# The first seven iterations of an attention and routing kernel, written out by hand

## The chip, the cores and the metric

The kernel runs on one core of a Trainium2 chip. The metric is the device time of one execution in microseconds (us), on the slowest core, here the only one. Five engines work side by side, each in the order of its own instruction stream: TensorE (PE in the rows, its weight loads PEld), VectorE (DVE), ScalarE (ACT), GpSimd (POOL), and SyncE (SP), which only issues DMAs. An instruction waits until what it reads is written and until the buffer it writes is free, and all behind it on its engine wait with it.

## The reference

Three layers run one after another. The change touches only the first, attention over pooled keys and values, for 8 batches of 8 heads, 576 tokens and 64 elements a head:

```python
k_p = k.reshape(B, H, Sp, pool, D).mean(axis=3)      # pool 8: 576 rows become 72
v_p = v.reshape(B, H, Sp, pool, D).mean(axis=3)
scores = scale * np.matmul(q, k_p.transpose(0, 1, 3, 2))
scores = scores - np.max(scores, axis=-1, keepdims=True)
attn = np.exp(scores)
attn = attn / (np.sum(attn, axis=-1, keepdims=True) + 1e-09)
attn_out = np.matmul(attn, v_p).astype(np.float32)
...
xn = x / (np.linalg.norm(x, axis=-1, keepdims=True) + 1e-06)
en = expert_emb / (np.linalg.norm(expert_emb, axis=-1, keepdims=True) + 1e-06)
logits = xn @ en.T / tau
expert_idx = np.argmax(logits, axis=1)
...
h = np.maximum(np.maximum(x @ w1, x @ w2), x @ w3)
out = h @ w_out
```

Its output, 4608 tokens of 512 elements, is routed: each token goes to the one expert of eight with the largest logit (a product with the normalised expert embedding `en`) and is weighted by a softmax over the logits. A dense layer follows.

## The kernel before

**Tiles and loop.** The tokens are cut into 36 tiles of 128, nine for two batches (four of the even batch, one mixed tile with half of each, four of the odd batch). The loop `for it in range(NT + 4)` (line 1607) runs a software pipeline over them. Its iteration `it` issues, in this order: the loads that are due; scores, maximum and subtraction of tile it-1 (`stage_s`, 449 to 491); the turned weights of tile it-3 (`stage_a`, 496: five transposes on TensorE, two copies on ScalarE); the turned queries of tile `it` (`stage_q`, 434, copied by ScalarE); the exponent of tile it-1 (`stage_e`, 492); the squares for the token's norm that are waiting in `squares` (line 557, ScalarE); the value products of tile it-4 and the output behind them on VectorE (`stage_x`, 516 to 557: reciprocal of the sum, the scaled output `x`, the logits `dt` and `lg`); and last the jobs that the table `todo` has for this iteration. All products are in fp32 and take two passes on TensorE.

**Keys and values.** `prep_steps(b)` (297) gives the jobs that prepare one batch. The raw rows lie as 72 x 8 = 576 rows in five chunks (four of 128 partitions, one of 72). The eight rows behind a pooled one are added, on VectorE by one reduction of a chunk (`pool_k`, 305; `pool_v1`, 313) or on GpSimd by three halving additions (`pool_k2`, 319; `pool_v`, 329). `dup_k` (323, ScalarE) copies the key sums beside themselves, `trans_k` (342) turns them on TensorE, and ScalarE copies them into a block `kbd` with zeros beside them (351, 352), one of three in turn. `spread_v` (335, GpSimd) writes the value sums into a block `vbd`, `trans_v` (372) turns them, and `vdot` (379, 386) multiplies them with the expert embedding, so that the value products yield the logits too. From batch 2 on the values lie beside the keys in the tile `kp`, and one transposition turns both (`trans_kv`, 359, with the copies 365 to 367).

**Loads.** `load_rows` (214) loads a batch's raw rows on SP's queue, `load_half` (204) half of them, and `add_half` (212) adds the other half to them by accumulating DMAs on GpSimd's queue, from batch 3 on. The raw tiles have one tag each, `kraw` and `vraw`, that hands its buffers round.

**What sets the order at the start.** Before the loop stand the key sums of batch 0 and their turning (`p0[0]()`, 1505). The norm of the expert embedding (`en_steps`, 1506) and constants for the routing (`const_steps`, 1545) are generators: `between` and `fill` draw one step of them at a time from a queue, in the gaps of VectorE's stream. The jobs of batches 0 to 2 are spread over the iterations by hand:

```python
todo = {0: [lambda: fill(16), p0[2]], 1: [lambda: fill(2), p0[3]], 2: [p0[4]], 3: [p0[5]], 5: [...const_steps...]}
at_ = {1: [2, 4, 6, 7], 2: [5, 6, 6, 7, 7, 7, 8, 9, 10]}.get(b, at_[:4] + at_[5:6])
```

So batch 2's first key sum goes out in iteration 5, the next two in 6, the last two and the spreading and turning from 7 on; batch 3's accumulating loads go out in iteration 4.

Of the kernel before, what the change touches and what calls it, by code (L numbers as in the profile page):

```python
# [21 lines left out]
def attention_moe_moe_kernel(  # L22
# [97 lines left out]
    if True:  # L120
# [61 lines left out]
        if True:  # L182
# [31 lines left out]
            def load_rows(pool_tag, src, b, sizes, apart=False, step=4):  # L214
                t = kvp.tile([P, 5, J, D], F32, tag=pool_tag, name=f"{pool_tag}{b}")
# [74 lines left out]
            for c, (h0, h1) in enumerate(HS[:4]):  # L290
                nc.gpsimd.tensor_copy(mslot[:, SL[c] : SL[c + 1], 0], rmask[:, c, h0:h1])
            for i in range(3):
                if i > 0:
                    nc.gpsimd.memset(kbds[i], 0.0)
                nc.gpsimd.tensor_scalar(vbds[i][:, :, D : D + 1], mslot, float(J), None, A.mult)

            def prep_steps(b):
# [8 lines left out]

                def pool_all():
                    for c in range(5):
                        pool_k(c)
# [20 lines left out]

                def spread_v():
                    for c, (h0, h1) in enumerate(HS):
                        n = RC[c]
                        sh = [n, h1 - h0, D]
                        nc.gpsimd.tensor_tensor(
                            vb[0:n, SL[c] : SL[c + 1], 0:D],
                            vp[0:n, c : c + 1, :].to_broadcast(sh),
                            mslot[0:n, SL[c] : SL[c + 1], :].to_broadcast(sh),
                            op=A.mult,
                        )  # L340

                def trans_k(cs, h0, h1):
# [50 lines left out]
                if b == 0:  # L393
                    return [
                        lambda: (pool_all(), dup_k(), trans_k(range(4), 0, 7), trans_k([4], 7, 8)),
                        lambda: (pool_v(2, 4, P), pool_v(4, 5, R4)),
                        lambda: pool_v1(0),
                        lambda: (pool_v1(1), spread_v()),
                        lambda: (trans_v(0, 4), trans_v(4, 5)),
                        lambda: vdot(),  # L400
                    ]
                if b == 1:
                    return [
                        lambda: (pool_k(0), pool_k(1), pool_k2(RC, 2), pool_v(0, 4, P), pool_v(4, 5, R4)),
                        lambda: (dup_k(), spread_v(), trans_k(range(4), 0, 7), trans_k([4], 7, 8)),
                        lambda: (trans_v(4, 5), trans_v(0, 4)),
                        vdot,
                    ]
# [25 lines left out]
            def stage_q(i):  # L434
# [4 lines left out]
                for c in range(4):  # L439
# [5 lines left out]
                    nc.tensor.transpose(ps[:, c * P : (c + 1) * P], blk_, ident)  # L445
                nc.scalar.copy(qT, ps.rearrange("p (c n) -> p c n", n=P))
                st_q[i] = qT

            def stage_s(i):
                m, part, t, segs = tiles[i]  # L450
                qT = st_q.pop(i)
                ps = pb.tile([P, 2, 512], F32, tag="psc", name=f"psc{i}")
                if part == 1:
# [62 lines left out]
            def stage_x(i):  # L516
                m, part, t, segs = tiles[i]
                aT = st_a.pop(i)
                ps = pb.tile([P, 2, 512], F32, tag="pav", name=f"pav{i}")
                for bank in range(2):  # L520
# [53 lines left out]
            uses = {}  # L574

            def uname(name):
                uses[name] = uses.get(name, 0) + 1
                return f"{name}_{uses[name]}"

# [924 lines left out]
            nc.scalar.activation(esq, en, AF.Square, accum_out=ess)  # L1504
            p0[0]()
            def en_steps():
                en2 = yield from inverse_norm(ap1, ess, E, 1, "en")
                vs(en, en, en2[:, 0:1], A.mult)
                yield
                ps = pq.tile([P, 512], F32, tag="pq", name="pe0")  # L1510
# [75 lines left out]

            queue.append([chain(en_steps())])
# [13 lines left out]
            qneed = {0: 0, 1: 4, 2: 5}  # L1601
            qnext = 3
            kvnext = 2
            cur = {}
            MA = NT1 + 3
            first = run(range(NREQ), between)
            for it in range(NT + 4):
                boundary()
# [9 lines left out]
                if it == NT:  # L1618
                    sq_.close()
                    open_b()  # L1620
                while qnext < len(qorder) and qorder[qnext][0] * 9 + qneed[qorder[qnext][1]] - 4 <= it:
                    load_q(*qorder[qnext])
                    qnext += 1
                while kvnext < B and kvnext * 4.5 - 11 <= it:
                    if kvnext < NFULL:
                        kv[kvnext] = (load_rows("kraw", k, kvnext, RC), load_rows("vraw", v, kvnext, RC))
                    else:
                        kv[kvnext] = (load_half("kraw", k, kvnext), load_half("vraw", v, kvnext))
                    kvnext += 1
                if 0 <= it - 1 < NT:  # L1630
# [15 lines left out]
                if it == NT + 1:  # L1646
                    next(first)
                for job in todo.get(it, []):
                    if callable(job):
                        job()  # L1650
                        continue
                    b, j = job
                    if b not in cur:
                        cur[b] = prep_steps(b)
                    cur[b][j]()
                if it == NT - 1 and started:
# [350 lines left out]
```

## Time and profile before

| | before |
|---|---|
| runs, median of 3 | 1204.89 us (1204.51 to 1204.91) |
| the profiled execution, its own time | 1203.55 us |
| its span, first to last instruction | 1201.4 us |
| mean granted clock of TensorE (1 is full) | 0.997 |
| TensorE busy | 1175.2 us (98%) |
| VectorE busy | 873.2 us (73%) |
| ScalarE busy | 606.8 us (51%) |
| GpSimd busy | 297.4 us (25%) |

The time of an execution is 2.15 us longer than its span. The attention covers only the start of the span, and the edited iterations some 50 us of it; an average over the span says nothing of them, so what matters there is read from timelines and short stretches. Busy time of TensorE is modelled at the ends of its matmuls, and grouped rows of matmuls overlap their neighbours a little; from one start to the next is the better measure of what a group takes.

### The profile page before, as it was taken

To read this page: it belongs to the slowest core of one execution; us is meant where nothing else is said; L and a number is where in the kernel's file an instruction comes from. 1 tells how busy PE (TensorE), PEld (TensorE's weight loads), DVE (VectorE), ACT (ScalarE), POOL (GpSimd) and SP (SyncE) were. 2 spreads that over 40 slices of the span, in tenths; PEclk is the share of its full clock that TensorE was granted. 3 is DMA by queue.
4 is the path that set the end of the run, shared out by engine and by line. 5 is a ranking of instruction groups with operands and counts; after the bars stand their busy time and mean duration, and the time that the engine had idled before them with its cause. 6 is when DMAs were issued, how large, how long until landed. Compare 5 with 4: busy or idle time off the path is not lost.

```text
span 1201.4 us, 23859 instructions
## 1 busy us (share of the span) xinstructions
PE 1175.2 (98%) x8761; PEld 1161.6 (97%) x8761; DVE 873.2 (73%) x1811; ACT 606.8 (51%) x1118; POOL 297.4 (25%) x462
## 2 busy tenths in 40 slices
PE   5999999999999999999999999999999999999997
PEld 4899999999999999999999999999999999999997
DVE  6878977978799999988765468468467557567563
ACT  4667674545666666666655244334334334334332
POOL 7978634001222122221201301103104004004001
PEclk9999999999999999999999999999999999999999
DMA  9899656328874457554939668877878877878873
GB/s 294 238 270 253 175 172 220 111 21 239 268 251 177 153 176 238 200 206 135 345 110 323 231 252 302 302 263 290 318 258 287 307 271 281 298 287 284 287 258 141
DMA packets 108121, 285.11 MB, mean 237 GB/s; under 512 B 17879, under 2 KB 70565, under 8 KB 97629
## 3 DMA queue, kind: packets, MB, share of 16 engines
q1 hardware_dynamic: 87436, 216.40, 51.8%
q0 software_dynamic: 20560, 67.11, 17.9%
q8 instruction: 71, 1.16, 0.4%
q14 instruction: 54, 0.43, 0.1%
HBM read 285.52 MB, written 52.48 MB: 281 GB/s over the span
## 4 chain that ended last, share of the span: by engine, by line
PE 92%; DVE 3%; ACT 2%; issue 1%; POOL 0%; DMA 0%; SPq 0%; POOLq 0%; DVEq 0%; ACTq 0%
PE p L1752 33%; PE ph L1097 17%; PE py L1158 17%; PE o L1864 10%; PE pav L524 3%; PE psc L470 2%; PE ph L1105 2%; PE py L1142 2%; PE px L1051 1%; PE paT L501 1%; PE pqT L445 1%; DVE sh L488 1%; DVE kp L305 1%; PE pd L379 1%; POOL out_dram L1872 0%
## 5 line engine op out<-in xcount | busy, mean ns | idle before, releaser
L1752 PE MATMUL p<-yhi,wt 128*128 128x384 f32 x1512 | 387.4, 336 | 0.1
L1752 PEld LDWEIGHTS p<-yhi,wt 128*128 128x128 f32 x1512 | 273.4, 188 | 0.3 <-issue 0.3
L1752 PE MATMUL p<-ylo,wt 128*128 128x384 f32 x756 | 254.1, 336 | 0.0
L1760 ACT COPY s<-p 128x384 f32<-128x384 f32 x162 | 77.6, 479 | 200.7 <-PE p L1752 200.7
L1158 PE MATMUL py<-hhi,whi 128*128 128x256 f32 x576 | 164.6, 286 | 0.0
L1097 PE MATMUL ph<-xhi,wlo 128*128 128x256 f32 x576 | 163.1, 283 | 0.5 <-DVE wlo L1077 0.5
L1097 PE MATMUL ph<-xhi,whi 128*128 128x256 f32 x576 | 163.5, 284 | 0.0
L1097 PE MATMUL ph<-xlo,whi 128*128 128x256 f32 x576 | 163.0, 283 | 0.0
L1158 PE MATMUL py<-hhi,wlo 128*128 128x256 f32 x576 | 162.9, 283 | 0.0
L1158 PE MATMUL py<-hlo,whi 128*128 128x256 f32 x576 | 162.9, 283 | 0.0
L1752 PEld LDWEIGHTS p<-ylo,wt 128*128 128x128 f32 x756 | 142.2, 188 | 0.0
L1864 PE MATMUL o<-wt,ghi 128*128 128x256 f32 x756 | 136.2, 282 | 0.0
L1779 DVE TENSOR_TENSOR blk<-p,s 128x384 f32<-128x384 f32 x108 | 59.6, 552 | 88.8 <-PE p L1752 88.8
L1737 POOL DMA_INDIRECT gt<-gbuf,ix x26 | 33.9, 1304 | 337.9 <-DMA ix<-idbuf 267.9
L1864 PEld LDWEIGHTS o<-wt,ghi 128*128 128x128 f32 x756 | 116.7, 188 | 0.9 <-DVE m L1780 0.8
L1097 PEld LDWEIGHTS ph<-xhi,wlo 128*128 128x128 f32 x576 | 110.5, 192 | 0.7 <-DVE wlo L1077 0.7
L1097 PEld LDWEIGHTS ph<-xhi,whi 128*128 128x128 f32 x576 | 110.5, 192 | 0.0
L1097 PEld LDWEIGHTS ph<-xlo,whi 128*128 128x128 f32 x576 | 110.5, 192 | 0.0
L1158 PEld LDWEIGHTS py<-hlo,whi 128*128 128x128 f32 x576 | 110.5, 192 | 0.0
L1158 PEld LDWEIGHTS py<-hhi,whi 128*128 128x128 f32 x576 | 110.4, 192 | 0.0
L1158 PEld LDWEIGHTS py<-hhi,wlo 128*128 128x128 f32 x576 | 110.4, 192 | 0.0
L1077 DVE TENSOR_TENSOR wlo<-w2raw,whi 128x1024 fp32r<-128x1024 f32 x86 | 105.1, 1225 | 6.9 <-ACT whi L1068 6.8
(345 smaller groups left out, 2348.6 us busy)
## 6 DMA issues: line engine op xcount, KB each, us to landing
wt<-wdram SPq DMA_DIRECT2D x69, 1792.0 KB
w1raw<-in_moe_w_dram SPq DMA_DIRECT2D x88, 512.0 KB
w2raw<-in_moe_w_dram SPq DMA_DIRECT2D x88, 512.0 KB
wdram<-wst POOLq DMA_DIRECT2D x9, 1792.0 KB, 6.6
ybuf<-yo SPq DMA_DIRECT2D x40, 256.0 KB
cvraw<-in_moe_w_dram POOLq DMA_DIRECT2D x36, 256.0 KB, 4.4
xbuf<-x SPq DMA_DIRECT2D x16, 512.0 KB
yr<-ybuf SPq DMA_DIRECT2D x20, 384.0 KB
```

The lines of the kernel that those rows point to most:

```text
L470: nc.tensor.matmul(ps[:, c // 2, (c % 2) * 2 * SP : (c % 2 + 1) * 2 * SP], qT[:, c, :], kbds[segs[0][2] % 3][:, h0 + c].rearrange("p t s - ...
L524: nc.tensor.matmul(ps[lo:hi, bank, (g0 % 4) * DA : (g0 % 4 + g1 - g0) * DA], aT[:, c, lo:hi], vbds[b % 3][:, sl : sl + g1 - g0, :].rearran ...
L1077: nc.vector.tensor_tensor(lo, src, hi.bitcast(F32), op=A.subtract)
L1097: nc.tensor.matmul(ps[:, f, :], a_[:, c, fs], b_[:, c, :], start=(n == 0), stop=(n == 3 * DC - 1))
L1105: nc.tensor.matmul(ps[:, f, 0:P], tl["w1"][piece][:, c, fs], xlo[:, c, 0:P], start=(c == 0), stop=(c == DC - 1))
L1142: nc.tensor.matmul(ps[h], a_[:, f, 0:P], b_[:, f, cols], start=(piece == 0 and f == 0 and n == 0), stop=(last_ and f == 1 and n == 2),)
L1158: nc.tensor.matmul(py[:, c // 2, (c % 2) * 256 : (c % 2 + 1) * 256], a_[:, f, c * P : (c + 1) * P], b_[:, f, :], start=(piece == 0 and f = ...
L1737: nc.gpsimd.indirect_dma_start(out=gt[g][:, j : j + 1], out_offset=None, in_=gbuf[:, :], in_offset=bass.IndirectOffsetOnAxis(ap=cols[j], a ...
L1752: nc.tensor.matmul(ps, a_, b_, start=(start and c + n == 0), stop=(c == 1 and n == 2), skip_group_check=True)
L1760: nc.scalar.copy(t, ps)
L1779: tt(src, add[0], add[1], op=A.add)
L1864: nc.tensor.matmul(ps, a_, b_, start=(m in (1, 2, 5) and c + n == 0), stop=(c == KH - 1 and n == 2), skip_group_check=True,)
```

## The change

The loop now begins at iteration 8. Iterations 0 to 7 are written out as straight calls, in another order: tiles 0 and 2 are scored first, then 1 and 3; the query copy of tile 0 goes to VectorE; the steps of the embedding norm are issued between the key sums of batch 0; GpSimd adds chunks 1 and 4 of batch 0's keys, VectorE the fifth value chunk of batch 0; batch 1's sums and products come at other places. A new helper `turn(n)` issues n products of the identity with itself, whose result nothing reads. Batch 2's key sums go out two with tile 6's iteration and three in iteration 8, its turned keys in 9; batch 3's accumulating loads in iteration 8; the routing constants from iteration 11. On SP's queue the keys of batch 1 stand before the mixed queries, its values before the third group of queries. The raw tiles have tags by even and odd batch, with one buffer each.

```diff
-                t = kvp.tile([P, 5, J, D], F32, tag=pool_tag, name=f"{pool_tag}{b}")
+                t = kvp.tile([P, 5, J, D], F32, tag=f"{pool_tag}{b % 2}", name=f"{pool_tag}{b}_", bufs=1)
...
+            kv[1] = [load_rows("kraw", k, 1, RC)]
             load_q(0, 1)
-            kv[1] = [load_rows("kraw", k, 1, RC)]
+            kv[1].append(load_rows("vraw", v, 1, RC))
             load_q(0, 2)
-            kv[1].append(load_rows("vraw", v, 1, RC))
...
+            def turn(n):
+                ps = pb.tile([P, 2, 512], F32, tag="pav", name=uname("turn"))
+                for _ in range(n):
+                    nc.tensor.matmul(ps[:, 0, 0:P], ident, ident, start=True, stop=True)
...
-                def pool_all():
-                    for c in range(5):
+                def pool_all(between):
+                    pool_one(1)
+                    pool_one(4)
+                    for c, n in ((0, 5), (2, 11), (3, 0)):
+                        for _ in range(n):
+                            next(between, None)
                         pool_k(c)
...
                 if b == 2:
-                    pk = [lambda: (pool_k(0), pool_v(0, 4, P), pool_v(4, 5, R4)), *(lambda c=c: pool_k(c) for c in range(1, 5))]
+                    pk = [lambda: (pool_v(0, 4, P), pool_v(4, 5, R4))]
+                    pk += [lambda c0=c0: [pool_k(c) for c in range(c0, min(c0 + 2, 5))] for c0 in (0, 2, 4)]
                     return pk + [spread_v, lambda: trans_kv(range(4), 0), lambda: trans_kv([4], 4 * P), vdot]
...
-                nc.scalar.copy(qT, ps.rearrange("p (c n) -> p c n", n=P))
+                copy = nc.vector.tensor_copy if i == 0 else nc.scalar.copy
+                copy(qT, ps.rearrange("p (c n) -> p c n", n=P))
...
-            todo = {0: [lambda: fill(16), p0[2]], 1: [lambda: fill(2), p0[3]], 2: [p0[4]], 3: [p0[5]], 5: [lambda: queue.append([chain(const_steps())])]}
+            todo = {11: [lambda: queue.append([chain(const_steps())])]}
...
-                at_ = {1: [2, 4, 6, 7], 2: [5, 6, 6, 7, 7, 7, 8, 9, 10]}.get(b, at_[:4] + at_[5:6])
+                at_ = {1: [], 2: [None, None, 8, 8, 9, 9, 9, 10], 3: [9, 10, 12, 13, 14]}.get(b, at_[:4] + at_[5:6])
                 if b >= NFULL:
-                    todo.setdefault(need - 9, []).append(
+                    todo.setdefault(8 if b == 3 else need - 9, []).append(
...
+            turn(22)
+            en_left = en_steps()
+            p0[0](en_left)
...
+            load_kv(2)
+            for _ in en_left:
+                pass
+            stage_q(0)
+            stage_q(2)
+            turn(3)
+            stage_s(0)
+            stage_s(2)
+            en_products()
+            p0[2]()
+            later_blocks(2, 3)
+            turn(12)
+            stage_e(0)
+            stage_e(2)
+            stage_q(1)
+            stage_q(3)
+            stage_s(1)
+            p0[3]()
+            stage_s(3)
+            stage_e(1)
+            p0[4]()
+            stage_a(0)
+            stage_e(3)
+            p1 = prep_steps(1)
+            p1[0]()
+            p1[1]()
+            stage_x(0)
+            stage_a(1)
+            stage_x(1)
+            stage_q(4)
+            stage_a(2)
+            p1[2]()
+            p1[3]()
+            stage_x(2)
+            kv[3] = [load_half("kraw", k, 3)]
+            load_q(1, 0)
+            stage_a(3)
+            stage_s(4)
+            stage_q(5)
+            sq_rest()
+            stage_x(3)
+            stage_s(5)
+            stage_e(4)
+            sq_rest()
+            stage_a(4)
+            stage_q(6)
+            cur[2] = prep_steps(2)
+            cur[2][1]()
+            kv[3].append(load_half("vraw", v, 3))
+            stage_s(6)
+            stage_e(5)
+            p1[4]()
+            cur[2][0]()
+            p1[5]()
+            stage_q(7)
+            stage_e(6)
+            for it in range(8, NT + 4):
```

The order of the instructions on TensorE, from its first one. `ptk0` are batch 0's turned keys, `pqT` turned queries, `psc` scores, `pe0` the turned embedding, a number behind them the tile. Before:

```order
L347 MATMUL ptk0_0_220<-ident_80,kp0_174 128x128 x3
L347 MATMUL ptk0_0_220<-ident_80,kp0_174 128x120
L347 MATMUL ptk0_7_227<-ident_80,kp0_174 128x72
L445 MATMUL pqT0_278<-ident_80,qgrp0_0_147 128x128 x4
L470 MATMUL psc0_307<-kbd0_166,qT0_279 128x144 x4
L1512 MATMUL pe0_315<-ident_80,en_139 64x8 x8
L445 MATMUL pqT1_327<-ident_80,qgrp0_0_147 128x128 x4
L470 MATMUL psc1_341<-kbd0_166,qT1_328 128x144 x4
```

The same place after the change:

```order
L309 MATMUL turn_1_209<-ident_80 128x128 x22
L372 MATMUL ptk0_0_264<-ident_80,kp0_174 128x128 x3
L372 MATMUL ptk0_0_264<-ident_80,kp0_174 128x120
L372 MATMUL ptk0_7_271<-ident_80,kp0_174 128x72
L486 MATMUL pqT0_321<-ident_80,qgrp0_0_147 128x128 x4
L486 MATMUL pqT2_328<-ident_80,qgrp0_0_147 128x128 x4
L309 MATMUL turn_2_335<-ident_80 128x128 x3
L512 MATMUL psc0_339<-kbd0_166,qT0_322 128x144 x4
L512 MATMUL psc2_349<-kbd0_166,qT2_329 128x144 x4
L1550 MATMUL pe0_359<-ident_80,en_139 64x8 x8
L309 MATMUL turn_3_379<-ident_80 128x128 x12
L486 MATMUL pqT1_394<-ident_80,qgrp0_0_147 128x128 x4
```

The `turn` products come in at three places, and tile 2 takes its place ahead of tile 1.

VectorE around the scores of tiles 7 and 8. `mx` and `sh` are maximum and subtraction of a tile, `rs4` to `lg` the output of tile 4, `kp0<-kraw2` key sums of batch 2. Before:

```order
L305 TENSOR_REDUCE kp0_174<-kraw2_272 128x64
L305 TENSOR_REDUCE kp0_174<-kraw2_272 72x64
L485 TENSOR_REDUCE mx7_725<-psc7_719 128x8
L488 TENSOR_TENSOR sh7_727<-psc7_719,mx7_725 128x576
L534 TENSOR_SCALAR rs4_759<-pav4_746 128x8
L536 RECIPROCAL rs4_759<-rs4_759 128x8
L544 TENSOR_TENSOR x4_762<-pav4_746,rs4_759 128x512
L549 TENSOR_TENSOR dt4_764<-pav4_746,rs4_759 128x64
L551 TENSOR_REDUCE lg_121<-dt4_764 128x8
L485 TENSOR_REDUCE mx8_785<-psc8_780 128x8
L488 TENSOR_TENSOR sh8_787<-psc8_780,mx8_785 128x576
```

The same place after the change:

```order
L527 TENSOR_REDUCE mx7_707<-psc7_701 128x8
L530 TENSOR_TENSOR sh7_709<-psc7_701,mx7_707 128x576
L576 TENSOR_SCALAR rs4_740<-pav4_727 128x8
L578 RECIPROCAL rs4_740<-rs4_740 128x8
L586 TENSOR_TENSOR x4_743<-pav4_727,rs4_740 128x512
L591 TENSOR_TENSOR dt4_745<-pav4_727,rs4_740 128x64
L593 TENSOR_REDUCE lg_121<-dt4_745 128x8
L319 TENSOR_REDUCE kp0_174<-kraw2__315 128x64 x2
L319 TENSOR_REDUCE kp0_174<-kraw2__315 72x64
L527 TENSOR_REDUCE mx8_771<-psc8_766 128x8
L530 TENSOR_TENSOR sh8_773<-psc8_766,mx8_771 128x576
```

The last key sums of batch 2, before tile 7's maximum until now, stand behind tile 4's output, and there are three of them.

ScalarE around the exponent of tile 4 (`atm4<-sh4`). `sq` are squares, `aT` copies of turned weights. Before:

```order
L446 COPY qT5_520<-pqT5_519 128x512
L494 ACTIVATE atm4_506<-sh4_509 128x576
L557 ACTIVATE sq0_472,ssq_122<-x0_467 128x512
L503 COPY aT1_173<-paT3_575 128x512
L504 COPY aT1_173<-paT3_575 72x128
L446 COPY qT6_584<-pqT6_583 128x512
```

The same place after the change:

```order
L488 COPY qT5_595<-pqT5_594 128x512
L599 ACTIVATE sq2_566,ssq_122<-x2_561 128x512
L599 ACTIVATE sq1_521,ssq_122<-x0_493 128x512
L599 ACTIVATE sq0_498,ssq_122<-x0_493 128x512
L536 ACTIVATE atm4_589<-sh4_592 128x576
L599 ACTIVATE sq3_618,ssq_122<-x2_561 128x512
L545 COPY aT0_172<-paT4_632 128x512
L546 COPY aT0_172<-paT4_632 72x128
L488 COPY qT6_641<-pqT6_640 128x512
```

Three squares stand between tile 5's query copy and tile 4's exponent, and tile 4's turned weights follow that exponent directly.

## Rows read from the trace of the kernel before

**Rows 1.** The page, busy tenths of TensorE in 40 slices of 30 us.

```profile
PE   5999999999999999999999999999999999999997
```

**Rows 2.** Stretches: start:end, length, busy us PE PEld DVE ACT POOL, clock, DMA share, GB/s.

```profile
45.00:50.00 5.00, 3.95 (x19) 3.51 (x19) 5.00 (x22) 2.04 (x5) 4.49 (x10) 0.66 1.21 203
60.00:80.00 20.00, 19.41 (x169) 19.02 (x168) 15.71 (x48) 13.01 (x33) 13.59 (x30) 1.00 1.08 291
```

**Rows 3.** The chain that ended last, 0 to 60 us: start, us, what.

```profile
48.50 1.98 DVE kp L305 x2
...
56.27 1.25 PE psc L470 x8
```

**Rows 4.** Timeline of TensorE, first 17 us: start, us, operation, [idle before <-what ended it].

```profile
14.15 2.26 PE L470 MATMUL psc<-kbd,qT 128*128 128x144 f32 x8 [0.77 <-ACT qT L446]
16.34 0.59 PE L1512 MATMUL pe<-ident,en 8*64 8x8 f32 x8
```

**Rows 5.** Timeline of TensorE, 35 to 75 us.

```profile
35.68 1.19 PE L470 MATMUL psc<-kbd,qT 128*128 128x144 f32 x8
36.71 0.71 PE L501 MATMUL paT<-ident,at 128*128 128x128 f32 x5
37.26 0.60 PE L445 MATMUL pqT<-ident,qgrp 128*128 128x128 f32 x4
37.69 1.69 PE L524 MATMUL pav<-vbd,aT 128*128 128x146 f32 x12
39.21 0.71 PE L372 MATMUL ptv<-ident,vp 128*64 128x128 f32 x5
...
43.92 1.23 PE L379 MATMUL pd<-enT,vT 128*128 128x16 f32 x10
46.20 1.95 PE L470 MATMUL psc<-kbd,qT 128*128 128x144 f32 x8 [1.05 <-DVE sh L488]
...
50.00 1.60 PE L524 MATMUL pav<-vbd,aT 128*64 128x146 f32 x24
...
72.83 1.36 PE L456 MATMUL psc<-kbd,qT 128*64 128x144 f32 x16 [0.59 <-ACT qT L446]
```

**Rows 6.** Timeline of VectorE, 16 to 32 us.

```profile
16.45 0.76 DVE L485 TENSOR_REDUCE mx<-psc 128x8 f32<-128x576 f32 x1 [2.18 <-PE psc L470]
17.24 0.76 DVE L488 TENSOR_TENSOR sh<-psc,mx 128x576 f32<-128x576 f32 x1
...
29.90 0.17 DVE L534 TENSOR_SCALAR rs<-pav 128x8 f32<-128x8 f32 x1 [0.89 <-PE pav L524]
...
31.19 0.27 DVE L551 TENSOR_REDUCE lg<-dt 128x8 f32<-128x64 f32 x1
```

**Rows 7.** Timeline of ScalarE, 11 to 36 us.

```profile
11.06 0.57 ACT L351 COPY kbd<-ptk 64x504 f32<-64x504 f32 x1 [0.53 <-PE ptk L347]
...
23.27 0.69 ACT L374 COPY vT<-ptv 64x512 f32<-64x512 f32 x2
...
29.64 0.55 ACT L323 COPY kp<-kp 128x256 f32<-128x256 f32 x2
...
33.98 0.58 ACT L503 COPY aT<-paT 128x512 f32<-128x512 f32 x1 [1.57 <-PE paT L501]
34.46 0.26 ACT L504 COPY aT<-paT 72x128 f32<-72x128 f32 x1
...
35.09 0.70 ACT L494 ACTIVATE atm<-sh 128x576 f32<-128x576 f32 x1
35.68 0.63 ACT L557 ACTIVATE sq<-x 128x512 f32<-128x512 f32 x1
```

**Rows 8.** Timeline of GpSimd, 37 to 59 us.

```profile
37.56 2.38 POOL L212 DMA_DIRECT2D kraw<-in_k_dram  x2 [0.56 <-DVE lg L551]
...
50.31 0.45 POOL L319 TENSOR_TENSOR kraw<-kraw 128x128 f32<-128x128 f32 x1
...
58.14 0.31 POOL L329 TENSOR_TENSOR kp<-vraw 72x64 f32<-72x64 f32 x1
```

More of the change, by code (lines that the diff above doesn't have):

```diff
@@ L214, in load_rows @@
             def load_rows(pool_tag, src, b, sizes, apart=False, step=4):
[L215 removed]
+                t = kvp.tile([P, 5, J, D], F32, tag=f"{pool_tag}{b % 2}", name=f"{pool_tag}{b}_", bufs=1)
                 flat = src[b].rearrange("h (s j) d -> (h s) (j d)", j=J)
@@ L291, in attention_moe_moe_kernel, with later_blocks, uname @@
                 nc.gpsimd.tensor_copy(mslot[:, SL[c] : SL[c + 1], 0], rmask[:, c, h0:h1])
-            for i in range(3):
-                if i > 0:
+            nc.gpsimd.tensor_scalar(vbds[0][:, :, D : D + 1], mslot, float(J), None, A.mult)
+            def later_blocks(i0, i1):
+                for i in range(i0, i1):
                     nc.gpsimd.memset(kbds[i], 0.0)
-                nc.gpsimd.tensor_scalar(vbds[i][:, :, D : D + 1], mslot, float(J), None, A.mult)
+                    nc.gpsimd.tensor_scalar(vbds[i][:, :, D : D + 1], mslot, float(J), None, A.mult)
+            uses = {}
+            def uname(name):
+                uses[name] = uses.get(name, 0) + 1
+                return f"{name}_{uses[name]}"
+            def turn(n):
+                ps = pb.tile([P, 2, 512], F32, tag="pav", name=uname("turn"))
+                for _ in range(n):
+                    nc.tensor.matmul(ps[:, 0, 0:P], ident, ident, start=True, stop=True)
             def prep_steps(b):
@@ L305, in pool_k, with pool_one @@
                     nc.vector.tensor_reduce(kp[0:n, c, 0, :], kt[0:n, c].rearrange("p j d -> p d j"), axis=AX, op=A.add)
-                def pool_all():
-                    for c in range(5):
+                def pool_one(c):
+                    n = RC[c]
+                    for w in (4, 2, 1):
+                        dst = kt[0:n, c, 0:w, :] if w > 1 else kp[0:n, c, 0:1, :]
+                        nc.gpsimd.tensor_tensor(dst, kt[0:n, c, 0:w, :], kt[0:n, c, w : 2 * w, :], op=A.add)
+                def pool_all(between):
[4 more added lines that the diff above has]
+                            next(between, None)
                         pool_k(c)
@@ L329, in pool_v, with spread_v @@
                             nc.gpsimd.tensor_tensor(dst, vt[0:n, c, 0:w, :], vt[0:n, c, w : 2 * w, :], op=A.add)
-                def spread_v():
-                    for c, (h0, h1) in enumerate(HS):
+                def spread_v(order=range(5)):
+                    for c in order:
+                        h0, h1 = HS[c]
                         n = RC[c]
@@ L340, in spread_v, with trans_k0 @@
                         )
+                def trans_k0():
+                    for tag, c0, c1, h0, h1 in (("paT", 0, 4, 0, 7), ("psc", 4, 5, 7, 8)):
+                        ps = pb.tile([P, 2 * 512], F32, tag=tag, name=f"ptk0_{h0}")
+                        for c in range(c0, c1):
+                            n = KC[c]
+                            nc.tensor.transpose(
+                                ps[:, (c - c0) * P : (c - c0) * P + n],
+                                kp[0:n, c].rearrange("p two d -> p (two d)"),
+                                ident[0:n, 0:n],
+                            )
+                        n = (h1 - h0) * SP
+                        nc.scalar.copy(kb[0:D, h0:h1, 0, :], ps[0:D, 0:n].rearrange("p (h s) -> p h s", s=SP))
+                        nc.scalar.copy(kb[D:P, h0:h1, 1, :], ps[D:P, 0:n].rearrange("p (h s) -> p h s", s=SP))
                 def trans_k(cs, h0, h1):
@@ L394, in prep_steps @@
                     return [
[L395 to L398, printed above, removed]
+                        lambda between: (pool_all(between), dup_k(), trans_k0()),
+                        lambda: pool_v(2, 4, P),
+                        lambda: (pool_v1(0), pool_v1(1), pool_v1(4), spread_v((2, 3, 0, 1, 4))),
                         lambda: (trans_v(0, 4), trans_v(4, 5)),
-                        lambda: vdot(),
+                        vdot,
                     ]
@@ L403, in prep_steps @@
                     return [
-                        lambda: (pool_k(0), pool_k(1), pool_k2(RC, 2), pool_v(0, 4, P), pool_v(4, 5, R4)),
-                        lambda: (dup_k(), spread_v(), trans_k(range(4), 0, 7), trans_k([4], 7, 8)),
+                        lambda: (pool_k(0), pool_k(1)),
+                        lambda: (pool_k2(RC, 2), pool_v(0, 4, P), pool_v(4, 5, R4), spread_v()),
+                        dup_k,
+                        lambda: (trans_k(range(4), 0, 7), trans_k([4], 7, 8)),
                         lambda: (trans_v(4, 5), trans_v(0, 4)),
@@ L451, in stage_s @@
                 qT = st_q.pop(i)
-                ps = pb.tile([P, 2, 512], F32, tag="psc", name=f"psc{i}")
+                ps = pb.tile([P, 2, 512], F32, tag={1: "pav", 2: "paT"}.get(i, "psc"), name=f"psc{i}")
                 if part == 1:
@@ L518, in stage_x @@
                 aT = st_a.pop(i)
-                ps = pb.tile([P, 2, 512], F32, tag="pav", name=f"pav{i}")
+                ps = pb.tile([P, 2, 512], F32, tag="psc" if i == 1 else "pav", name=f"pav{i}")
                 for bank in range(2):
@@ L1585, in const_steps @@
                 yield
-            queue.append([chain(en_steps())])
+            later_blocks(1, 2)
             p0[1]()
-            todo = {0: [lambda: fill(16), p0[2]], 1: [lambda: fill(2), p0[3]], 2: [p0[4]], 3: [p0[5]], 5: [lambda: queue.append([chain(const_steps())])]}
+            todo = {11: [lambda: queue.append([chain(const_steps())])]}
             for b in range(1, B):
@@ L1606, in attention_moe_moe_kernel, with load_kv, loads @@
             first = run(range(NREQ), between)
-            for it in range(NT + 4):
+            def load_kv(n):
+                if n < NFULL:
+                    kv[n] = (load_rows("kraw", k, n, RC), load_rows("vraw", v, n, RC))
+                else:
+                    kv[n] = (load_half("kraw", k, n), load_half("vraw", v, n))
+            def loads(it):
+                while counts[0] < len(qorder) and qorder[counts[0]][0] * 9 + qneed[qorder[counts[0]][1]] - 4 <= it:
+                    load_q(*qorder[counts[0]])
+                    counts[0] += 1
+                while counts[1] < B and max(counts[1] * 4.5 - 11, 9) <= it:
+                    load_kv(counts[1])
+                    counts[1] += 1
@@ new lines, in jobs, with sq_rest @@
+            def jobs(it):
+                for job in todo.get(it, []):
+                    if callable(job):
+                        job()
+                        continue
+                    b, j = job
+                    if b not in cur:
+                        cur[b] = prep_steps(b)
+                    cur[b][j]()
+            def sq_rest():
+                while squares:
+                    squares.pop()()
+            counts = [4, 4]
+            load_kv(2)
+            for _ in en_left:
+                pass
@@ L1620, in attention_moe_moe_kernel @@
                     open_b()
[L1621 to L1629, printed above, removed]
+                loads(it)
                 if 0 <= it - 1 < NT:
@@ L1647, in attention_moe_moe_kernel @@
                     next(first)
[L1648 to L1655, printed above, removed]
+                jobs(it)
                 if it == NT - 1 and started:
```

8 lines of the change are left out of this document (1 added, 7 removed).

## Prediction

> **What bounds the kernel now.** I read the page's slices first. The reader is to see that the first of 40 slices has TensorE at 5 tenths and nearly all others at 9 [rows 1]: only the first 30 us or so have idle time to win, and past them a shift of TensorE's work moves the end by as much. The second view is the stretches: from 60 to 80 us TensorE is busy 19.41 of 20.00 us, but from 45 to 50 only 3.95 of 5.00, at a granted clock of 0.66, while VectorE is busy 5.00 of 5.00 [rows 2]. So up to about 52 us it is not TensorE that paces the tiles. The third view, the chain that ended last, says who does: sums of raw keys on VectorE (48.50, two in 1.98) stand in it, and the scores of tile 9 at 56.27 [rows 3]. I use those scores as the mark. At that point both programs have issued the same TensorE work (scores 0 to 8, value products 0 to 5, turned keys of batches 0 to 2, batch 2's value logits not yet), and from there they run the same loop, so the forecast is the start of tile 9's scores after the change, less 56.27.
>
> **The start, up to tile 1's queries.** Batch 0's keys arrive as before, and the copies of the first turned keys started at 11.06, so the keys were turned by 11.1 [rows 7]. The change gives two of the five key sums to GpSimd and hides the 16 small VectorE steps of the embedding norm before the keys arrive; the last chunk from DMA sets the time either way, so I keep 11.1 (bounds: 1 sooner, the price of one sum where two took 1.98 [rows 3], and 1 later, should a chunk of GpSimd, some 1.6 by the working below, be the last). Then, on the rows' warm durations: two key copies of 0.57 to 12.3, scores of tile 0 (1.19 [rows 5]) to 13.5, those of tile 2 behind ScalarE's query copy to 14.5, the embedding product (0.59, at 16.34, as the half-rate scores before it [rows 4]) to 15.1, 12 dummy products in 24 passes. One more pass of 128 columns costs 0.11 (0.71 for five, 0.60 for four [rows 5]), so 2.6, and tile 1's queries start at 17.7.
>
> TensorE's clock enters here. The eight passes of the scores at 14.15 took 2.26, the same eight at 35.68 took 1.19 [rows 4, 5]: the early ones ran at half rate, 1.2 of 2.4 GHz, though the clock column has no record of it. The 22 leading dummy products fill the idle time ahead of the first turned keys, and I take the later ones as warm. The Trainium skill, page "TensorE: Matmul & The Clock Gate" (Part 1), says the same in general: half rate is the default, and sustained activity, not any one instruction, lifts it; the rows at 14.15 and 35.68 agree.
>
> **From there to tile 9's scores**, the longest chain through the in-order engines, each step at its row [rows 3, 5, 6, 7]:
> - Queries 0.60, copy 0.58, scores 1.19, maximum and subtraction 2 x 0.76, exponent 0.70, transposes 0.71, copy 0.58 and the short last one: value products of tile 0 start at 23.7.
> - Value products 1.52 to the next start (37.69 to 39.21), transposes 0.71, copies 0.74: value products of tile 1 at 26.7. Another 1.52, queries of tile 4 0.43 to the next start, transposes 0.71, copies 0.74, then ScalarE's copies of batch 1's key sums 0.55, which stand behind them: turned keys of batch 1 at 30.7, the five passes of a transposition. TensorE does value products 2 and transposes 3 first: scores of tile 4 start at 33.3 and take 1.36. Here the new order is ahead by two value products.
> - Queries of tile 5 to 35.1, copy 0.58, then three squares of 0.63 on ScalarE, which the new order puts before tile 4's exponent: 37.6. Exponent 0.70, transposes 0.71, copies 0.74, query copy 0.58: scores of tile 6 at 40.3. Scores 1.19, batch 1's values turned 0.71, copied 0.69, multiplied 1.23, queries of tile 7 0.60, copy 0.58: scores of tile 7 at 45.3.
> - Scores 1.03 to the next start, transposes 0.55, queries 0.43, mixed value products of tile 4 1.60: 48.9. VectorE then has, in this order, tile 4's output (31.19 + 0.27 - 29.90 = 1.56), three key sums of batch 2 (3.0), and only then tile 8's maximum and subtraction (1.52): 55.0. ScalarE: exponent 0.70, square 0.63, two key copies 1.14: 57.5.
>
> The steps hand over some 28 times between engines; 0.03 to 0.04 each, as from the end of the scores at 16.41 to 16.45 and from the end of that, 16.45 + 0.76, to 17.24 [rows 4, 6], so 1.0 in all. Scores of tile 9 start at **58.5 against 56.27: 2.2 later**. The lead is lost in the last item: the key sums stand directly before the batch that needs them, so sum, turn, copy and score follow one another with nothing to run beside them. Before, the same sums ended at 50.48, and the turned keys had an iteration to spare.
>
> **The clock once more.** Before, TensorE waited 1.05 for VectorE at 46.20, and the eight score passes then took 1.95 instead of 1.19; the stretch shows 0.66 [rows 2, 5]. That is 5.00 x 0.34 = 1.7 of lost rate, already in 56.27. In the new order TensorE has done its value products and turned keys by about 54.5 and waits some 4 us for tile 9's keys, longer than the wait that preceded the fall before. Bounds: no fall, 0; one as before, 1.7; two, 3.5 (the value logits with their few columns, at about 43, preceded the fall before, too). I take one: 1.8 with its tail.
>
> **What costs nothing.** The constants' small steps leave VectorE's queue around 45 to 50 us for iterations 11 to 13, where TensorE is the bound and VectorE has 4.29 of 20.00 us free; should that cover go, they cost at most what VectorE did beside two key sums there, 5.00 - 1.98 = 3.0 [rows 2, 3]. Keys 1 and values 1 each go ahead of one load of queries on SP's queue; the queries behind them are first needed near 33 us. The accumulating loads of batch 3 left GpSimd's queue at 37.56, and now stand behind five chunks of batch 2's values. The ten half-size chunks of batch 3 took 58.14 + 0.31 - 50.31 = 8.1, and five full ones have as much to add: batch 3's sums end at 66.6 at most, instead of 58.45. Its keys are used in the mixed scores of tile 13, at 72.83 + 2.2, less 0.71 to turn them and three copies of 0.57: 72.6 [rows 5, 7, 8]. If GpSimd lost 6 us more, that would be the next wait. Tile and buffer names (even, odd) alone issue nothing.
>
> **Sum.** 2.2 + 1.8 = 4.0 later. The profiled execution took 1203.55 (span 1201.4 and 2.15 around it): 1207.55. The median of the runs is 1204.89, 1.34 above it, so **1208.9**.
>
> **The rivals.**
> - The lead holds (faster). At tile 4's scores the new order is ahead by two value products, 3.0. If TensorE paced the five tiles from there (3.5 each, as from the scores at 35.68 to the end of the value products at 39.21, and 0.71 + 1.23 + 0.71 for values turned, multiplied and keys turned [rows 5]), tile 9 would start at 33.3 + 17.5 + 2.7 = 53.5; with the old fall of the clock gone as well it gains 2.8 to 4.5, and with batch 1's key copies not held behind tile 2's, up to 6. I price it at -4: 1200.9. It decides where the three key sums end: it needs them before 50, not at 53.4. For it: TensorE's own work would allow 53.5; against it: the order on VectorE and ScalarE is fixed. 0.2.
> - It cancels (same). No fall of the clock, and the chain 1 us shorter than I add up, since neighbours on VectorE and ScalarE overlap by up to 0.1 where they don't depend: 0 to 2.4 later, 1206. 0.28.
> - The dummy products don't warm the clock (the change does not do what it says). Then everything from 11.1 to 17.7 takes up to twice as long: 2 x 1.1 for scores, 1.2 for queries, 2.6 for dummies, so 5 to 6 more; or the clock falls twice. 1210.7 to 1214. By the Trainium skill's same section an idle engine goes back to half rate, which speaks for a fall after each long wait; the trace agrees at 46.2. 0.12.
> - My forecast, 2.5 to 6 later: 0.40.
>
> **How the numbers follow.** A difference of 0.2% (2.4 us) is about what a measurement of this kernel can tell from none. Slower: 0.40 + 0.12 = 0.52. Same: 0.28. Faster: 0.20. The range reaches down to -4.4 (the faster rival's price and a little) and up to +7.1 (two falls, or the cold start in part): 1200.5 to 1212.0; beyond either end some 0.1 is left. The likeliest case alone would be 1207.4 to 1211.
>
> **What the profile would show.** Right: TensorE busy well before the first turned keys and the first scores of eight passes near 1.2 us long; value products of tile 0 near 24 and of tile 2 near 31; scores of tile 4 near 33 and of tile 9 near 58.5, after a wait of 3 to 4 us that ends with ScalarE's key copies; three key sums on VectorE between tile 4's output and tile 8's maximum; a stretch of clock below 1.00 soon after. Wrong: scores of tile 9 before 55, or a wait for GpSimd's sums, or early scores above 2 us.

## The result and the profile after

The changed kernel took 1210.97 us in the median of 5 runs (1210.02 to 1213.53), the kernel before 1204.91 (1204.51 to 1205.92): ratio 1.0053, 95% interval 1.0038 to 1.0068, so some 6 us slower, where 4.0 slower was forecast. The profiled execution took 1211.93, with a span of 1210.2 (before 1201.4).

The first slice of TensorE is fuller than before [rows 1]:

```profile
PE   8799999999999999999999999999999999999997
```

The stretches (start:end, length, busy us of PE, PEld, DVE, ACT, POOL, clock, DMA share, GB/s), to be held against [rows 2]:

```profile
45.00:50.00 5.00, 4.32 (x23) 3.72 (x24) 1.76 (x3) 1.92 (x4) 5.00 (x9) 0.66 0.71 108
55.00:60.00 5.00, 0.94 (x8) 0.54 (x6) 3.84 (x9) 2.35 (x6) 3.96 (x11) 1.00 0.66 184
60.00:65.00 5.00, 5.00 (x27) 4.95 (x28) 1.52 (x2) 2.95 (x8) 3.64 (x5) 0.66 0.97 298
```

TensorE does 0.94 us of work from 55 to 60, and there are two stretches at a clock of 0.66 where there was one. The fuller first slice is mostly the dummy products, whose result nothing reads. The chain that ended last (start, us, what) says what was waited for, where [rows 3] had sums at 48.50 and tile 9's scores at 56.27:

```profile
49.91 1.66 PE pav L566 x24
...
53.08 2.97 DVE kp L319 x3
56.05 0.68 DVE mx L527
...
56.82 0.77 DVE sh L530
57.61 0.68 ACT at L536
58.29 0.61 ACT sq L599 x2
58.91 0.46 ACT kbd L404
...
59.38 0.58 ACT kbd L405
...
60.00 2.04 PE psc L512 x8
```

Three key sums, tile 8's maximum and subtraction, its exponent, a square, two key copies, and only then tile 9's scores, 3.73 later than before. TensorE's timeline (start, us, operation, [idle before <-what ended it]), against [rows 4, 5]:

```profile
12.59 2.23 PE L512 MATMUL psc<-kbd,qT 128*128 128x144 f32 x16
...
19.16 1.25 PE L512 MATMUL psc<-kbd,qT 128*128 128x144 f32 x8 [0.24 <-ACT qT L488]
...
24.28 1.76 PE L566 MATMUL pav<-vbd,aT 128*128 128x146 f32 x12 [0.72 <-ACT aT L545]
...
33.98 1.20 PE L498 MATMUL psc<-kbd,qT 128*64 128x144 f32 x16
...
46.15 1.84 PE L512 MATMUL psc<-kbd,qT 128*128 128x144 f32 x8 [0.68 <-ACT qT L488]
...
51.45 1.25 PE L512 MATMUL psc<-kbd,qT 128*128 128x144 f32 x8
...
60.00 2.04 PE L512 MATMUL psc<-kbd,qT 128*128 128x144 f32 x8 [3.51 <-ACT kbd L405]
...
66.34 1.23 PE L512 MATMUL psc<-kbd,qT 128*128 128x144 f32 x8
...
97.62 0.66 PE L486 MATMUL pqT<-ident,qgrp 128*128 128x128 f32 x4 [0.31 <-ACT vT L406]
...
109.03 1.22 PE L512 MATMUL psc<-kbd,qT 128*128 128x144 f32 x8 [0.61 <-DVE rs L576]
...
119.93 1.76 PE L566 MATMUL pav<-vbd,aT 128*128 128x146 f32 x12 [0.40 <-DVE dt L591]
...
180.52 0.36 PE L1133 MATMUL ph<-xhi,whi 128*128 128x256 f32 x1
```

Of the kernel before, tile 10's scores and the first expert product:

```profile
60.95 1.23 PE L470 MATMUL psc<-kbd,qT 128*128 128x144 f32 x8
...
172.93 0.36 PE L1097 MATMUL ph<-xhi,whi 128*128 128x256 f32 x1
```

So the 8.8 us between the two profiled spans divide like this (some 2.3 of the difference between these two executions is their own spread: the kernel before was profiled at 1203.55, 1.36 below its median, the changed one at 0.96 above its median). Tile 9's scores come 3.73 later (60.00 against 56.27). From them to tile 10's it takes 6.34 instead of 4.68: 1.66, the fall of the clock. From tile 10 to the first expert product (180.52 against 172.93) it takes 114.18 instead of 111.98: 2.2, of which the waits at 97.62, 109.03 and 119.93, which the kernel before lacks, are 1.3. The last 1.2 lie behind that, where both kernels issue the same; the five runs differ by 3.5 among themselves, and I ascribe that part to nothing.

That the sums need not have stood where they stand is seen on VectorE, which was idle for 2.76 us some 5 us before:

```profile
45.02 0.25 DVE L425 TENSOR_TENSOR vbd<-pd,mslot 128x88 f32<-128x88 f32 x1 [0.88 <-PE pd L418]
48.03 0.76 DVE L527 TENSOR_REDUCE mx<-psc 128x8 f32<-128x576 f32 x1 [2.76 <-PE psc L512]
```

### The profile page after: what moved, and what is told of

The parts are those of the page before. It is cut to its first block, busy times and chain, and to the rows that moved or that the text cites. A ratio compares the mean times of both kernels' runs of the same rounds, so it can differ in the third digit from the quotient of the medians.

```text
span 1210.2 us, 24004 instructions
## 1 busy us (share of the span) xinstructions
PE 1184.2 (98%) x8835; PEld 1169.8 (97%) x8835; DVE 874.8 (72%) x1811; ACT 607.5 (50%) x1117; POOL 301.3 (25%) x465
## 4 chain that ended last, share of the span: by engine, by line
PE 92%; DVE 4%; ACT 2%; issue 1%; DMA 0%; POOL 0%; POOLq 0%; DVEq 0%; ACTq 0%
PE p L1862 33%; PE ph L1133 17%; PE py L1194 17%; PE o L1974 10%; PE pav L566 3%; PE psc L512 2%; PE ph L1141 2%; PE py L1178 2%; PE px L1087 1%; PE paT L543 1%; PE pqT L486 1%; PE pd L418 1%; DVE kp L319 0%; DVE x L586 0%; POOL out_dram L1982 0%
```

## The experiments

My theory: the late key sums hold tile 9, the clock falls behind that wait, and the late constants cost TensorE's waits further on. The rivals: the loss lies in the new start (order of tiles, dummy products), or in the phase of GpSimd and DMA. Each row of the table is one kernel; the last two columns are lengths from its own timeline (start to start), since the first scores start anywhere from 12.6 to 14.2 and ran at half rate for a part in some. Each ratio is to runs of the kernel before taken along with that kernel's; each length is from one profiled execution. In some of these the clock fell at tile 7, which is worth some 1.6 of the first length: before, changed, e3 (there from tile 6 on, and more), e7, e8 and e12 have that fall in them, the others not. Those with the old order of tiles (before, e7, e10, e11) compare with each other.

| kernel | ratio to before (95%) | tile 1's scores to tile 9's | tile 9's to first expert product |
|---|---|---|---|
| before | 1 | 37.62 | 116.66 |
| changed | 1.0053 (1.0038 to 1.0068) | 40.84 | 120.52 |
| e1 sums early | 1.0012 (1.0003 to 1.0021) | 36.32 | 118.73 |
| e2 sums and turned keys early | 1.0001 (0.9992 to 1.0010) | 35.18 | 117.50 |
| e3 constants early | 1.0083 (1.0070 to 1.0097) | 45.38 | 119.28 |
| e4 squares later | 1.0035 (1.0022 to 1.0049) | 38.50 | 119.84 |
| e5 no dummies | 1.0046 (1.0032 to 1.0060) | 39.45 | 120.75 |
| e6 dummies in the wait | 1.0029 (1.0018 to 1.0040) | 39.19 | 117.93 |
| e7 before, with dummies | 1.0016 (1.0005 to 1.0026) | 39.07 | 116.76 |
| e8 combined | 1.0009 (0.9997 to 1.0021) | 38.16 | 117.03 |
| e9 keys, squares, constants | 0.9986 (0.9977 to 0.9995) | 34.48 | 117.68 |
| e10 before, late sums | 1.0028 (1.0018 to 1.0039) | 39.00 | 120.08 |
| e11 before, late constants | 0.9980 (0.9971 to 0.9988) | 36.07 | 117.71 |
| e12 same as e9, copies early | 0.9987 (0.9978 to 0.9996) | 35.07 | 118.86 |

**The key sums (e1, e2, e10).** e1 issues them in VectorE's idle time (and takes them out of the table `at_`, not shown):

```diff
             p1[5]()
+            cur[2][2]()
+            cur[2][3]()
             stage_q(7)
```

> The three last key sums of batch 2 go out behind batch 1's value logits, where VectorE was idle from 45.27 to 48.03 us; the turned keys stay in iteration 9. Theory (late sums hold tile 9): sums end near 48.3, tile 9's scores start at 57.5 instead of 60.00, their copies still behind tile 8's exponent; about 1208 us. Rival (the loss lies in the early order of tiles and the dummy products): tile 9 moves by under 0.5 us, 1211 us.

e2 also turns the keys in iteration 8 (`2: [None, None, None, None, 9, 8, 8, 10]`).

> As the one before, and the turned keys of batch 2 in iteration 8. Theory: tile 9's scores near 55.6, no wait over 1.5 us ahead of them and so no fall of the clock behind them (1.7 back): about 1205 us, 6 less than the changed kernel. Rival (sums alone matter, the fall has another cause): no more than the run with the sums alone, or clock 0.66 again after 55 us.

Timelines of e1, VectorE and TensorE:

```profile
45.18 2.93 DVE L319 TENSOR_REDUCE kp<-kraw__315 128x64 f32<-128x512 f32 x3
48.04 0.74 DVE L527 TENSOR_REDUCE mx<-psc 128x8 f32<-128x576 f32 x1
...
46.15 1.25 PE L512 MATMUL psc<-kbd,qT 128*128 128x144 f32 x8 [0.67 <-ACT qT L488]
...
49.83 1.25 PE L512 MATMUL psc<-kbd,qT 128*128 128x144 f32 x8
...
55.50 1.25 PE L512 MATMUL psc<-kbd,qT 128*128 128x144 f32 x8 [1.37 <-ACT kbd L405]
```

TensorE did not wait for the sums there: they end at 48.11, some 0.7 behind the end of tile 7's scores, so that tile 7's maximum waits for them, but tile 8's scores follow tile 7's in 3.68, as they do in e6, where the sums stand late. Tile 9 starts at 55.50, 4.5 earlier; 2.5 were expected, and most of the rest is a fall of the clock at tile 7 that this run lacks (below). e2 reaches tile 9 at 55.84, from first scores 0.7 later than in e1, with no wait ahead of it. The ratios fall to 1.0012 and 1.0001: undoing this one place takes back nearly the whole loss. What else the change moved (loads, buffer tags, the order of tiles) was not tried piece by piece; e2 shows that all of it together is worth at most 0.1% either way. The other way round, e10 puts three of the sums late in the kernel before, and with them the spreading and turning that follow them (`2: [5, 6, 8, 8, 8, 9, 9, 9, 10]`), and changes nothing else.

> The kernel before with three of batch 2's key sums in iteration 8 behind tile 4's output and their turning in iteration 9, as the change has them, and nothing else. Theory (this order alone makes the loss): tile 9's scores 57 to 58 instead of 56.27, behind a wait of over 2 us on ScalarE's key copies, clock below 1.00 behind it: 2 to 4 slower. Rival (only together with the other edits): within 1 of before.

```profile
44.39 1.23 PE L470 MATMUL psc<-kbd,qT 128*128 128x144 f32 x8
...
57.38 2.29 PE L470 MATMUL psc<-kbd,qT 128*128 128x144 f32 x8 [3.51 <-ACT kbd L366]
```

The same wait to the hundredth, the slow scores behind it, and 1.0028. The new order of tiles and the dummies are not needed for this wait and this fall. But 1.0028 is about half of 1.0053. In part that is because the kernel before waited 1.05 at tile 7 with a fall of the clock behind it [rows 5], and e10, with one sum instead of two ahead of tile 6's maximum, has neither (44.39); what makes up the rest is not shown.

**The clock (e6).** Dummies fill the wait, in the loop at `it == 10` ahead of `stage_s(9)`: `turn(14, "paT")`.

> 14 more products of the identity in TensorE's queue directly ahead of tile 9's scores, where it waited 3.51 us. Theory (that wait is what the clock falls after): tile 9's scores at 60.0 as before, but 1.2 instead of 2.04 us long, tile 10's scores 1.7 earlier than 66.34, clock 1.00 from 60 to 65; about 1209.3 us. Rival (the fall comes by itself): clock 0.66 there again, 1211 us.

TensorE's timeline of e6:

```profile
56.20 3.29 PE L309 MATMUL turn<-ident 128*128 128x128 f32 x28
59.87 1.25 PE L512 MATMUL psc<-kbd,qT 128*128 128x144 f32 x8 [0.38 <-ACT kbd L405]
...
64.54 1.23 PE L512 MATMUL psc<-kbd,qT 128*128 128x144 f32 x8
```

Tile 9 comes at nearly the same time as in the changed kernel, which is chance (tile 1's scores were 1.52 later here, and the clock did not fall at tile 7). But tile 10 follows in 4.67 instead of 6.34: the fall behind the wait is gone, 1.67 as expected. The ratio went down by 0.0024, or 2.9 us, more than that; the two intervals allow it.

**The dummies at the start (e5, e7).** e5 leaves out all three groups of `turn`.

> The changed kernel without the products of the identity (22, 3 and 12 of them left out; nothing reads their result). Theory (they lift the clock before the first scores): the eight passes of the first scores near 2.2 us instead of 1.1 to 1.25, value products of tile 0 about 2.5 us later than 24.28, tile 9's scores later by about as much: 1213 us. Rival (they only keep TensorE from its work): tile 1's queries 2.9 us earlier than 17.89, 1208 us.

e7 adds 22 of them to the kernel before, ahead of `p0[0]()`.

> The kernel before, with 22 products of the identity ahead of the first turned keys and nothing else changed. Theory (the warm start is a gain that the rest of the change then loses): first scores 1.2 us instead of 2.26, value products of tile 0 3 to 5 us earlier than 28.17, of which VectorE's key sums and constants let through 1 to 3 at tile 9: 1202 to 1204 us. Rival (VectorE paces all up to 52 us): tile 9 within 0.5 us of 56.27, 1205 us.

TensorE in e5, then in e7:

```profile
13.33 2.70 PE L512 MATMUL psc<-kbd,qT 128*128 128x144 f32 x16
...
19.35 1.25 PE L512 MATMUL psc<-kbd,qT 128*128 128x144 f32 x8 [1.93 <-ACT qT L488]
```

```profile
9.84 1.06 PE L347 MATMUL ptk<-ident,kp 128*128 128x128 f32 x5 [1.06 <-ACT kp L323]
11.80 0.66 PE L445 MATMUL pqT<-ident,qgrp 128*128 128x128 f32 x4 [0.90 <-ACT kbd L352]
13.22 2.26 PE L470 MATMUL psc<-kbd,qT 128*128 128x144 f32 x8 [0.77 <-ACT qT L446]
```

Both of my expectations fell. Without dummies the sixteen passes took 2.70 instead of 2.23, so the clock rose during them, and tile 1's scores started at 19.35 instead of 19.16: ScalarE's query copy set that, not TensorE. The ratio is 1.0046, not to be told from 1.0053. In the kernel before, the dummies ended at 8.78, three waits of 1.06, 0.90 and 0.77 followed, and the first scores took 2.26 as ever: what the dummies had gained of the clock was gone behind these waits (from 15 to 20 us the granted clock was 0.50). Tile 9 came 0.53 later, at 56.80, and the ratio is 1.0016: no gain.

**The squares (e4).** The four stand in ScalarE's gaps behind batch 1's turned values and tile 6's exponent (both `sq_rest()` go, two `squares.pop()()` follow `p1[4]()`, the rest `stage_e(6)`).

> The four squares that stood around tile 4's exponent go out in ScalarE's gaps behind batch 1's turned values and tile 6's exponent. Theory (they lie on the chain): tile 4's turned weights at 38.2 instead of 39.15, tile 7's scores 1.0 earlier than 46.15, tile 9's 1.0 earlier than 60.00; 1210 us. Rival (the chain is held by VectorE there): under 0.3 us at tile 7.

```profile
40.80 1.22 PE L512 MATMUL psc<-kbd,qT 128*128 128x144 f32 x8 [1.27 <-DVE sh L530]
...
45.68 1.25 PE L512 MATMUL psc<-kbd,qT 128*128 128x144 f32 x8 [0.68 <-ACT qT L488]
...
57.90 2.26 PE L512 MATMUL psc<-kbd,qT 128*128 128x144 f32 x8 [3.50 <-ACT kbd L405]
```

Between the two: from tile 1's scores, which started 0.24 later here, tile 7 gains 0.7, not 1.0, because VectorE's subtraction becomes the wait at tile 6 (1.27). Tile 9 is 2.1 earlier than in the changed kernel, but 1.6 of that is the fall at tile 7 that this run lacks. 1.0035, whose interval overlaps that of the changed kernel.

**The constants (e3, e8, e11, e9).** e3 queues them behind tile 1's value products, the place of before.

> The routing constants are queued behind tile 1's value products, as before the change, instead of in iteration 11. Theory (they push the first ranking steps against the later tiles): tile 9's scores within 0.5 us of 60.0, TensorE's waits for VectorE between 97 and 120 us gone, the first expert product 2 us earlier than at 180.52; about 1209 us. Rival (these waits come from GpSimd and DMA in another phase): waits stay, 1211 us.

e8 queues them ahead of tile 0's output, together with e2's and e4's edits.

> The changed kernel with the key sums of batch 2 and their turning early, the four squares in ScalarE's gaps, and the constants queued ahead of tile 0's output, where VectorE waits for value products (1.44 and 2.90 us idle). Theory: tile 9's scores 1 earlier than the 55.84 of the run with the keys alone, TensorE's waits for VectorE between 90 and 105 us (0.65 and 0.31 there) gone: 1203.5 us, 1 to 2 faster than the kernel before. Rival (the constants delay tile 4 as they did behind tile 1's value products): tile 9 at 57 or later, 1207 us.

e3's VectorE and TensorE:

```profile
35.60 2.22 DVE L623 TENSOR_SCALAR cc<-tokid 128x36 f32<-128x36 f32 x1
...
38.09 1.76 PE L566 MATMUL pav<-vbd,aT 128*128 128x146 f32 x12 [1.63 <-DVE ca L617]
...
65.24 2.29 PE L512 MATMUL psc<-kbd,qT 128*128 128x144 f32 x8 [3.51 <-ACT kbd L405]
```

The theory was half right. TensorE's waits of 0.31 and 0.61 are gone from the later part, and tile 9 to the expert products is 1.2 shorter; but in the changed order the constants stand in the outputs of tiles 2 and 3, for which the value products wait, and that costs 4.5 ahead of tile 9, falls of the clock among it. In e8 one of them still does it (1.77 of wait at tile 3's value products), and tile 9 comes at 57.54, as that run's rival said. e11 tries the late constants alone, in the kernel before.

> The kernel before with the constants queued in iteration 11 instead of 5, and nothing else. Theory: VectorE is rid of some 3 us of small steps up to 48 us, tile 9's scores 1 to 2.5 earlier than 56.27; but the first ranking steps meet later tiles, and TensorE waits 0.5 to 2 for VectorE between 85 and 105 us: in all within 1 of before. Rival (late constants cost nothing): no such waits, 1.5 to 2.5 faster.

```profile
44.44 1.22 PE L470 MATMUL psc<-kbd,qT 128*128 128x144 f32 x8 [0.21 <-DVE rs L534]
...
53.66 1.25 PE L470 MATMUL psc<-kbd,qT 128*128 128x144 f32 x8 [0.29 <-ACT qT L446]
...
89.17 0.66 PE L445 MATMUL pqT<-ident,qgrp 128*128 128x128 f32 x4 [0.31 <-ACT vT L367]
...
100.02 1.22 PE L470 MATMUL psc<-kbd,qT 128*128 128x144 f32 x8 [0.43 <-DVE rs L534]
```

The late waits come with the late constants here too (0.31 and 0.43, and the way to the experts is 1.05 longer), but tile 9 is 1.5 earlier and the clock didn't fall at tile 7: 0.9980, faster than before, where I expected no difference. So the late place is the better one in both orders (e3, with the constants early, is slower than the changed kernel): ahead of tile 9 TensorE waits for VectorE's outputs and less work there pays 1.5 and 4.5 (falls of the clock included), behind it the constants cost 1.05 and 1.2. e9 has e2's and e4's edits and the constants at iteration 8.

> The changed kernel with batch 2's key sums and turning early, the four squares in ScalarE's gaps, and the constants queued at the end of iteration 8 instead of 11. Theory (three causes, each undone): tile 9's scores 0.7 earlier, from the start of tile 0's scores, than the 42.54 of the run with the keys alone; no waits of TensorE on VectorE's reciprocal or on the value copy between 90 and 105 us; about 1203.5 us beside 1205, ratio 0.998 to 0.999. Rival (the late waits come without the constants): 0.65 and 0.31 of wait there again, ratio 1.000.

0.9986. Tile 9 is 0.70 sooner than in e2, as expected; but what the constants give back behind it is lost beside them (a wait of 0.29 at 56.32), 117.68 against 117.50. e12 also moves ScalarE's copies of batch 1's key sums ahead of tile 4's queries and tile 2's turned weights (`p1[2]()` moved up).

> As the first run of these four, and ScalarE's copies of batch 1's key sums ahead of tile 2's turned weights, in its idle time from 27.1 to 29.57. Theory (batch 1's turned keys waited 1.20 for them at 31.22): tile 4's scores 0.9 earlier, tile 9's 0.5 to 0.9 earlier; ratio 0.997 to 0.999. Rival (something else is late next): under 0.3 at tile 9.

From tile 1's scores, tile 4's came after 13.86 instead of e9's 14.82, 0.96 earlier, where 0.9 was expected, and the 1.2 wait is gone; but the clock fell at tile 7 in this run (2.29), so tile 9 doesn't show it, and neither does the ratio (0.9987). Undecided. e9, e11 and e12 take 0.1 to 0.2% less than the kernel before and some 0.7% less than the changed one, and are not told apart.

## Why the prediction was right, and where it was off

- **Slower, by the key sums' place: right, and shown** by e1, e2 and e10. The chain forecast 58.5 for tile 9. It came at 60.00, and 1.6 of that is a fall of the clock at tile 7: in the changed kernel tile 8's scores follow tile 7's in 5.30 (46.15 to 51.45), in e1 and e6 in 3.68. Without it 58.4. The steps on the way were each 0.6 to 0.9 early (tile 0's value products 23.7 for 24.28, tile 4's scores 33.3 for 33.98, tile 7's 45.3 for 46.15), in part because I took the hand-overs as one lump at the end.
- **The clock, "I take one: 1.8": the mis-sized term.** The profiled run has two falls, 1.62 at tile 7 and 1.66 at tile 9. Two, 3.5, was my upper bound. The second is the one I argued for, and e6 shows that it hangs on the wait.
- **The constants, "should that cover go, at most 3.0", taken as 0: wrong.** They pushed the ranking steps behind them to later tiles, where VectorE has less to spare; the waits are 1.2 longer in sum (4.5 against 3.3 from 66 us, in the kernel before 61, to the expert products), 2.2 with the small gaps. e3 gives back 1.2 there and e11 puts on 1.05, so that much belongs to the constants; that all 2.2 do isn't shown. The move as a whole was still right: their early place costs more in the new order (e3).
- **The sum, 4.0:** nearer to the 6.1 between the medians than to the 8.8 between the profiled spans, from which its rows come. Part of that nearness is luck, the spread of single executions.
- **The squares: right in kind**, 0.7 of the 1.9 that I put on the chain (e4).
- **Batch 3's sums**, taken as no cost: right. They ended at 59.39 and nothing waited for them.
- **The rivals.** "The lead holds" did not happen, but its point of decision was right: with the sums ended by 50 (e1, at 48.1) the loss is nearly gone. Its price was not: no gain of 4 appeared, e1 and e2 only come back to about the kernel before. "The dummies don't warm the clock": they did here, and in e7 not up to the first scores, and leaving them out makes no difference that can be measured (e5).

## What to carry to other kernels

Before moving work on an engine that is not the bound, look for the row in which that engine waits longest and put the work there; the same three sums held TensorE up nowhere when they stood in a 2.76 us idle time, and cost some 5 us one iteration later. Ask of every long wait of TensorE what the clock does behind it, and price that too. Work taken off an engine pays where that engine is the one waited for, and costs where it lands on a stretch in which it is waited for too, as the constants show in both orders.

## What the runs showed of the hardware

The fall of the clock behind a short wait is not settled by the order of the program. Nine of these kernels waited 0.67 or 0.68 for tile 7's queries after the value logits; in three (the changed kernel, e8, e12) the scores behind it took 1.84 to 2.29, in six (e1, e2, e4, e5, e6, e9) 1.25. (e3 waited as long too, but there the clock had fallen at tile 6 already.) The changed kernel and e6 issue the same up to there on every engine; TensorE's rows of the changed kernel and of e1 agree to 0.02 us from the first scores to there. One profile therefore does not show what a kernel always does at such a place. Behind the wait of 3.5 ahead of tile 9 it fell in all five kernels that had no dummies in it.

A small VectorE operation can take more than ten times its time. In e8 a scaling of 13 elements took 2.45, while GpSimd multiplied its five blocks of values and began the additions behind them, beside 0.19 for the same one in the kernel before; e3's 2.22 above is another, at the same place of GpSimd's work. VectorE's and GpSimd's rows of e8, then of the kernel before:

```profile
34.99 2.45 DVE L621 TENSOR_SCALAR gix<-iof 1x13 f32<-1x13 f32 x1
```

```profile
34.81 1.93 POOL L360 TENSOR_TENSOR vbd<-vp,mslot 128x128 f32<-128x128 f32 x5
36.70 1.24 POOL L353 TENSOR_TENSOR vraw__318<-vraw__318 128x256 f32<-128x256 f32 x2
```

```profile
48.18 0.19 DVE L585 TENSOR_SCALAR gix<-iof 1x13 f32<-1x13 f32 x1
```

```profile
47.08 1.27 POOL L329 TENSOR_TENSOR vraw<-vraw 128x256 f32<-128x256 f32 x2
```

The Trainium skill, page "SBUF — State Buffer" (section "SBUF: two separate sides"), says that VectorE in its faster modes and GpSimd share a pair of ports, that the one that starts first keeps it for its whole instruction, and that the other stands still. The rows of e8 look like such a stop, but it lasted through the five multiplications (34.81 to 36.74) and not through one instruction, and in the kernel before GpSimd's additions were running too when the scaling took 0.19. No run here was made to test it.
